# Attention with 32 narrow heads: the joined row maxima transposed one pair of units later, and the last units played four at a time

## Chip, cores and metric

The kernel runs on one core of one Trainium2 chip. The metric is device time of one execution in microseconds (us); smaller is better. Each time named "median" is over three executions of the same program.

## What is computed

A transformer block on one sequence of S = 2048 rows and D = 512 columns, all in float32: attention with 32 heads of width 16, then a gated MLP with a 2048 x 2048 mixing matrix. Only the first part bears on the change:

```python
h = x + A(layernorm(x))            # attention with a full softmax
h2 = h + B(layernorm(h))           # gelu, layernorm, w_sp @ z2, gate, w_out
# A: q, k, v = split(x @ wqkv) into 32 heads of 16 columns
scores = einsum("bhqd,bhkd->bhqk", q, k) * 16 ** -0.5
o = einsum("bhqk,bhkd->bhqd", softmax(scores), v)
return o @ wo
```

## The kernel before, in words

Everything before the line `with ExitStack() as at` (L673) projects x to q, k and v and writes them to scratch memory in DRAM; everything after L872 is the end of the attention's output product for most rows and the MLP. Between them lies the attention proper, on which the change works.

**Units and pairs.** A *unit* is four heads (one `hg` of 8), 512 queries (one `qb` of 4) and 128 keys (one `kb` of 16): 8 x 4 x 16 = 512 units in all. The loop at L826 takes two units at a time, a *pair*. Sixteen units, 8 pairs, share one `hg` and `qb`; I call them a *group* (g = 0 to 31) and number its pairs by their *place*, 0 to 7. A unit needs two score tiles of 128 x 1024, each from two matmuls that sit in the two halves of TensorE's rows (`scores_of`, L688, matmul L700), one exponential per tile on ScalarE (L706), and then `weigh` (L711, matmul L717): the product of the exponentials with v, four heads side by side in the four column strips of TensorE, added into the one PSUM bank `pv`. After the 16th unit `gather` (L721) copies `pv` out and sends it off with eight DMAs.

**Maxima.** The softmax subtracts the row maximum. It is not subtracted on an engine: two extra rows of the queries' tile `qst[g]`, rows 48 and 49 of each half, hold the negated maximum in two parts, two rows of ones stand against them in `kst`, and so the score matmul (50 rows deep) yields scores with the maximum already taken off. So no score matmul of group g can run before these rows are in `qst[g]`. They are made well ahead, by `max_pair` (L215): per step 8 matmuls (L233) into three PSUM banks, six reductions (L238) and one combined reduction (L247) on VectorE, and one absolute value (L243) on ScalarE. Eight such steps make the maxima of one group; one step goes into each pair but for places 0 and 1, of which the first is given two and shares them with the second. LEAD = 11 steps are made before the loop, so the pair at place 4 of group g holds the eighth step of group g+1.

When the eighth step is done, `end` (L249) joins the maxima: one reduction on VectorE (L251), and a split into two parts on GpSimd (L98, L101). Later `max_rows` (L273) transposes the parts on VectorE (L277) and writes them into `qst` with eight small DMAs issued by SyncE (L281).

**The order inside a pair** is written out by hand and carried out by `play` (L740). Its engines take their work strictly in the order in which it is written (manual schedule, L825). In the strings (L41 to L44) two S are one score tile: the first issues the matmul of the first row half, the second that of the other half and the exponential. h is one half (256 queries) of the `weigh` of the unit before, V the `weigh` of the pair's first unit, G the `gather`. M, m, v and u with a bank number are steps of the maxima. N runs `end`, if one has been left over by the pair before (`pending`, `ending`); T runs `max_rows`, if `end` has left something in `turned`. Places 0 and 1 use `FIRST_TWO`, which has no N and no T, the very first pair uses `START`, all others `ORDER`.

**The last units.** From n = 490 on there are no maxima left to make. These 11 pairs (L848 to L860) are not played from a string: two score tiles, `weigh` of the unit before, two score tiles, two or three matmuls of h (L635, `more_h`, with all 128 rows and columns of TensorE), `weigh` of the pair's first unit. The 24 matmuls of h belong to the output product of the first two blocks of 128 rows; `load_o` fetches the attention's output for one such block, `split_o` splits it in two parts. The maxima's three PSUM banks are free by then and serve as a third score tile and the accumulator of h (L842 to L844).

Of the kernel before, what the change touches and what calls it, by code (L numbers as in the profile page):

```python
# [19 lines left out]
S = 2048  # L20
D = 512
H = 32
# [4 lines left out]
NB = S // P  # L27
# [10 lines left out]

ORDER = "v2 S S M1 N S h m0 S m1 M2 S S h S M0 u1 T S V M0".split()  # L41
START = "S S S S M2 m1 h v0 M2 S S M1 S S M0 u2 V m0".split()
FIRST_TWO = ["v2 S S M1 S h S m2 M0 h G M1 S S m2 S m0 S V".split(),
             "u2 S S M1 m0 S S h h v2 M1 S S M0 S S M2 u1 V M0".split()]  # L44
# [12 lines left out]
def block_kernel(ctx: ExitStack, tc: tile.TileContext, x, wqkv, wo, w_in, w_sp4, b_sp, w_out, out):  # L57
# [109 lines left out]
    def head(hg, p, t):  # L167
        return 8 * (hg // 2) + 4 * t + 2 * (hg % 2) + p
# [117 lines left out]
    with ExitStack() as pre:  # L286
# [190 lines left out]
        with tc.manual_schedule(engines={E.PE, E.Activation, E.DVE, E.SP}):  # L477
# [91 lines left out]
            for j in range(24):  # L569
                b, n, i = 1 + j // 8, j // 2 % 4, 1 - j % 2  # L570
# [37 lines left out]
    h_rows = [0, 1, 2, HB, HB + 1, HB + 2] + [sb + HB * i for sb in range(3, HB) for i in range(2)]  # L608
    os_, o2s, xrs, hns, hTs = {}, {}, {}, {}, {}

    def load_o(sb):

        c = slice(sb * P, (sb + 1) * P)
        o = e2.tile([P, DB, P], F32, name="o")
        nc.sync.dma_start(o, o_scr[:, c].rearrange("(d p) s -> p d s", p=P))
        rc = e2.tile([P, DB, P], F32, name="rc")
        for d in range(DB):
            nc.sync.dma_start(rc[:, d, :], r_scr[8 * d:8 * d + 8, c].rearrange(
                "h (o s) -> h o s", o=1).to_broadcast([8, DH, P]))
        xrs[sb] = e2.tile([P, D], F32, name="xr", bufs=3)  # L620
        nc.sync.dma_start(xrs[sb], x[c, :])
        nc.gpsimd.tensor_mul(o, o, rc)
        os_[sb] = o

    def split_o(sb, eh="act", el=None):
        o = os_.pop(sb)
        o2s[sb] = [e2.tile([P, DB, P], F32R, name=f"o2{i}", bufs=1) for i in range(2)]
        split(o2s[sb][0], o2s[sb][1], o, eh, el)
# [44 lines left out]
    with ExitStack() as at:  # L673
# [14 lines left out]
        def scores_of(hg, qb, kb, p):  # L688

            q, k = qst[hg * NQ + qb], kst[hg % 2]
            turn[0] += len(later)
            pool = later[0] if later and turn[0] % 3 == 2 else ps_s
            s = pool.tile([P, 2, 512], F32, name="s")

            def product(t):
                r = slice(RG * t, RG * t + KM)
                nc.tensor.matmul(s[:, t, :], k[r, p, kb * P:(kb + 1) * P], q[r, p, :],  # L700
                                 start=True, stop=True)

            def second():
                product(1)
                t = pp.tile([P, 2, 512], F32, name="pt")
                nc.scalar.activation(t, s, AF.Exp, scale=DH ** -0.5)  # L706
                return t

            return lambda: product(0), second

        def weigh(hg, qb, kb, pts, cols=slice(0, 512)):  # L711

            if kb == 0:
                pv[0] = ps_v.tile([P, 512], F32, name="pv")
            for j in range(4):
                c = (4 * kb + j) * VW
                nc.tensor.matmul(pv[0][32 * j:32 * j + 32, cols], vst[hg % 2][:, c:c + 32],  # L717
                                 pts[j % 2][:, j // 2, cols], start=kb == 0,
                                 stop=kb == NB - 1 and cols.stop == 512)

        def gather(hg, qb, pool=sm):  # L721

            o = pp.tile([P, 512], F32, name="o", bufs=1)
            if pool is sm and not later:
                nc.scalar.activation(o, pv[0], AF.Copy)
            else:
                nc.vector.tensor_copy(o[:, :256], pv[0][:, :256])
                if later and pool is sm:
                    nc.vector.tensor_copy(o[:, 256:], pv[0][:, 256:])
                else:  # L730
                    nc.scalar.activation(o[:, 256:], pv[0][:, 256:], AF.Copy)
            cols = slice(qb * 512, (qb + 1) * 512)
            sums = pool.tile([P, 16], F32, name="sums")
            for j in range(4):
                h = head(hg, j % 2, j // 2)
                nc.sync.dma_start(o_scr[h * DH:(h + 1) * DH, cols], o[32 * j:32 * j + DH, :])
                nc.sync.dma_start(sums[32 * j:32 * j + 32, :], o[32 * j + DH:32 * j + VW, :])
            sums_[0] = (hg, cols, sums, pool)

        def play(order, prev, unit):  # L740
# [38 lines left out]
            assert not ending and len(pts) == 4  # L779
            played.append(pts[2:])  # L780

        played, pending = [], []
        steps_of = {kind: [] for kind in "Mmvu"}

# [17 lines left out]
        def more_h(k):  # L802

            for _ in range(k):
                if not pieces:
                    sb = h_rows[len(hns)]
                    acc = later[0].tile([P, 512], F32, name="h")
                    pieces.extend([sb, acc, h_products(sb, acc)])
                sb, acc, products = pieces
                next(products)  # L810
                made[0] += 1
                if made[0] % (3 * DB):
                    continue
                pieces.clear()
                add_h(sb, acc)
                split_o(h_rows[len(hns) + 1], *("pool", "pool") if hns else [None])
                mv, rs = scale_h(sb)
                hns[sb] = e2.tile([P, D], F32, name="hn", bufs=3)
                nc.vector.tensor_scalar(hns[sb], xrs.pop(sb), mv[:, 0:1], rs,
                                        op0=ALU.subtract, op1=ALU.mult)  # L820

        made = [0]
        units = [(hg, qb, kb) for hg in range(HG) for qb in range(NQ) for kb in range(NB)]
        prev, turn, later = None, [2], []
        with tc.manual_schedule(engines={E.PE, E.Activation, E.DVE, E.SP}):  # L825
            for n in range(0, len(units), 2):  # L826
                (hg, qb, kb), (_, _, kb1) = units[n:n + 2]
                if hg + 1 < HG and n % 64 < 24 and n % 4 == 0:
                    load_k(hg + 1, [n % 64 // 4])
                if hg + 1 < HG and n % 64 < 12 and n % 4 == 2:  # L830
                    load_uv(hg + 1, [n % 64 // 4])
                if hg + 1 < HG and n % 64 == 30:
                    load_v(hg + 1)
                if kb == 2 and n // NB + 3 < HG * NQ:
                    load_q(n // NB + 3)
                steps, place = n // 2 + LEAD < 8 * HG * NQ, n % NB // 2
                while m < min(8 * HG * NQ, n // 2 + LEAD + 1 + (not place and n > 0)):
                    for kind, some in max_pair(m, True).items():
                        steps_of[kind].extend(some)
                    m += 1  # L840
                if not steps and not later:
                    maxima.close()  # L842
                    later.append(attn.enter_context(
                        tc.tile_pool(name="ps_l", bufs=1, space=PSUM, side="right")))  # L844
                if steps:
                    play(START if not n else FIRST_TWO[place] if place < 2 < n else ORDER, prev, (hg, qb, kb, kb1))
                    pts1 = played.pop()
                else:  # L848
                    if pending:
                        pending.pop()()  # L850
                    pts = [score(hg, qb, kb, 0), score(hg, qb, kb, 1)]
                    weigh(*prev)
                    if kb == 0:
                        gather(*units[n - 1][:2])
                    pts1 = [score(hg, qb, kb1, 0), score(hg, qb, kb1, 1)]
                    if n >= 490:
                        more_h(2 + (n < 494))
                    weigh(hg, qb, kb, pts)
                    if turned:
                        max_rows()  # L860
                prev = (hg, qb, kb1, pts1)
                if kb == 6 and n > NB:
                    invert()
                if n % 32 == 16 and n < 6 * 32:
                    load_weights(n // 32)
                if n in (476, 482, 492, 504):
                    load_o(h_rows[(476, 482, 492, 504).index(n)])
                if n == 482:
                    split_o(h_rows[0], "pool", "pool")
            weigh(*prev)  # L870
            gather(*prev[:2], e2)
# [6 lines left out]
    def quarter(pool, name, tag):  # L878
        return pool.tile([P, HB, PITCH], F32R, name=name, tag=tag)[:, :, :FC]

    T = {n: [quarter(zc, n, f"{n}_{i}") for i in range(2)]
         for n in ("t3", "t2", "n4", "t1")}
# [175 lines left out]
    with ExitStack() as fin:  # L1058
# [41 lines left out]
        for p in range(HB):  # L1100
# [98 lines left out]
            if last:  # L1199
                t = zc.tile([P, HB * PITCH], F32, name="qz", tag="n4_1")  # L1200
                first = (t[:, :3 * FC].rearrange("p (i c) -> p i c", c=FC),
                         [t[:, (3 + 2 * i) * FC:(5 + 2 * i) * FC] for i in range(2)])
# [91 lines left out]
        prev, nxt = None, (first[0], None, first[1])  # L1294
        for p in range(HB):
            (q, _, z1), last = nxt, p + 1 == HB
            nxt = None if last else fetch(p + 1)
            h = fetch_h(p)
# [55 lines left out]
            prev = top  # L1354
# [36 lines left out]
```

## Time and profile before

| | |
|---|---|
| median of 3 executions | 1857.24 us (1857.11 to 1857.51) |
| the profiled execution | 1857.51 us |
| its span, first to last instruction | 1855.7 us |
| TensorE (PE) busy | 1846.0 us, 99% of the span |
| VectorE (DVE) busy | 1517.2 us, 82% |
| ScalarE (ACT) busy | 1363.0 us, 73% |
| GpSimd (POOL) busy | 226.4 us, 12% |
| granted TensorE clock | 1.000 of full speed |

Times in the views are microseconds from the span's start. PE is TensorE's matmuls, PEld its weight loads, SPq the queue of SyncE, which issues nearly all DMAs; a DMA row on SPq shows the time in which SyncE issues it, not its transfer. "out<-in" names the tile written and those read; "x8" says that eight instructions are merged in the row, and the second number is then the time from the first one's start to the last one's end. A bracket at the end of a row is idle time of that engine just before, and what ended it. Matmuls overlap: the time from one start to the next is what a matmul costs, not its duration. The chain of work is a list of pieces with start and length that follow on each other without a gap, back from the last instruction; a piece is what the end was waiting for at that time.

### The profile page before, as it was taken

Reading aid. Unit: us, or ns where it says so; the run is one execution under the profiler, and the core shown is the slowest. Engines: PE = TensorE matmul, PEld = TensorE weight load, DVE = VectorE, ACT = ScalarE, POOL = GpSimd, SP = SyncE. Lnnn points to the kernel's source line nnn. Section 1 sums busy time; section 2 is a strip of 40 time slices with the busy share of each in tenths; the row PEclk is TensorE's granted clock in tenths of the full one; section 3 lists DMA queues with packets and bytes.
Section 4 is the critical chain, followed back from the end, with each engine's and each line's share of the span. In section 5 each row is a group of like instructions: output and inputs, shape, how many; then the busy total and the mean of one; then the engine's idle time right before and its main releaser. Section 6 shows DMA issues by size and latency. Waiting matters only on the chain.

```text
span 1855.7 us, 35988 instructions
## 1 busy us (share of the span) xinstructions
PE 1846.0 (99%) x13362; PEld 1024.9 (55%) x13362; DVE 1517.2 (82%) x3030; ACT 1363.0 (73%) x1696; POOL 226.4 (12%) x305
## 2 busy tenths in 40 slices
PE   9999999999999999999999999999999999999999
PEld 6776333433334333334333333333437889999998
DVE  6487999999999999999999999999935777877664
ACT  3224999999999999999999999999995444434221
POOL 2241000011010100000000000000000756001111
PEclk9999999999999999999999999999999999999999
DMA  6688111221120121022011112100124554768662
GB/s 190 181 204 200 42 25 28 50 54 29 39 56 17 48 46 25 14 52 40 14 39 36 21 31 49 25 14 14 32 54 116 172 161 167 226 187 263 210 195 90
DMA packets 148759, 160.15 MB, mean 86 GB/s; under 512 B 63096, under 2 KB 93320, under 8 KB 147240
## 3 DMA queue, kind: packets, MB, share of 16 engines
q1 hardware_dynamic: 143800, 146.44, 29.6%
q10 hardware_dynamic: 4752, 11.41, 1.6%
q8 instruction: 105, 1.72, 0.4%
q14 instruction: 70, 0.57, 0.1%
q0 software_dynamic: 32, 0.01, 0.0%
HBM read 101.26 MB, written 55.61 MB: 85 GB/s over the span
## 4 chain that ended last, share of the span: by engine, by line
PE 97%; DVE 1%; ACT 1%; issue 1%; POOL 0%; POOLq 0%; DVEq 0%; ACTq 0%
PE pv L717 29%; PE m L233 22%; PE s L700 15%; PE acc L104 5%; PE acc L106 5%; PE acc L105 5%; PE g L106 4%; PE g L105 4%; PE g L104 4%; PE acc L635 2%; PE tp L1263 1%; PE h L635 0%; PE tp L959 0%; PE acc L1284 0%; PE acc L463 0%
## 5 line engine op out<-in xcount | busy, mean ns | idle before, releaser
L238 DVE TENSOR_REDUCE mx<-m 128x1 f32<-128x512 f32 x1508 | 949.4, 682 | 97.7 <-PE m L233 74.1
L706 ACT ACTIVATE pt<-s 128x1024 f32<-128x1024 f32 x1024 | 1012.8, 1022 | 15.2 <-PE m L233 6.0
L717 PE MATMUL pv<-pt,vst 128*32 128x256 f32 (+1 forms) x6048 | 591.6, 466 | 0.0
L233 PE MATMUL m<-kst,qst 48*128 48x512 f32 x1508 | 580.7, 468 | 0.5
L700 PE MATMUL s<-qst,kst 50*128 50x512 f32 x2048 | 567.8, 426 | 0.4 <-ACT pt L706 0.4
L233 PEld LDWEIGHTS m<-kst,qst 48*128 48x128 f32 x1508 | 236.6, 184 | 344.9 <-DVE mx L238 292.6
L700 PEld LDWEIGHTS s<-qst,kst 50*128 50x128 f32 x2048 | 271.8, 184 | 135.5 <-ACT pt L706 87.1
L717 PEld LDWEIGHTS pv<-pt,vst 128*32 128x32 f32 x6048 | 122.3, 108 | 230.6 <-issue 218.3
L233 PE MATMUL m<-uvs,qst 48*128 48x512 f32 x497 | 227.8, 458 | 0.0
L243 ACT ACTIVATE ab<-m 128x512 f32<-128x512 f32 x248 | 148.2, 598 | 77.3 <-PE m L233 76.5
L247 DVE CUSTOM_DVE_ANT_0 ab<-m,ab 128x512 f32<-128x512 f32 x249 | 169.4, 680 | 10.6 <-ACT pt L706 10.2
L98 POOL CAST mparts<-nm 128x16 fp32r<-128x16 f32 x32 | 6.3, 196 | 885.1 <-DVE nm L251 885.1
L233 PEld LDWEIGHTS m<-uvs,qst 48*128 48x128 f32 x497 | 90.9, 183 | 38.6 <-DVE mx L238 37.5
L899 ACT ACTIVATE ws<-a 128x512 fp32r<-128x512 f32 x80 | 45.8, 621 | 49.3 <-PE g L106 23.8
L978 ACT ACTIVATE z<-acc 128x464 f32<-128x464 f32 (+2 forms) x64 | 27.5, 456 | 62.5 <-PE acc L106 62.5
L104 PE MATMUL acc<-wi,hT 128*128 128x464 f32 (+2 forms) x196 | 72.8, 371 | 0.0
L106 PE MATMUL acc<-wi,hT 128*128 128x464 f32 (+2 forms) x196 | 71.8, 366 | 0.0
L105 PE MATMUL acc<-wi,hT 128*128 128x464 f32 (+2 forms) x196 | 71.6, 365 | 0.0
L900 DVE TENSOR_TENSOR ws<-a,ws 128x512 fp32r<-128x512 f32 x80 | 56.6, 749 | 12.2 <-ACT ws L899 11.9
L96 ACT ACTIVATE part<-acc 128x512 fp32r<-128x512 f32 x32 | 19.1, 596 | 60.9 <-PE acc L106 56.3
L104 PE MATMUL g<-b,ws 128*128 128x344 f32 x192 | 62.6, 326 | 0.0
L899 ACT ACTIVATE ws<-s 128x512 fp32r<-128x512 f32 x32 | 19.4, 631 | 57.7 <-DVE s L919 57.7
(201 smaller groups left out, 2157.2 us busy)
## 6 DMA issues: line engine op xcount, KB each, us to landing
a<-in_w_sp SPq DMA_DIRECT2D x80, 256.0 KB
qst<-q_scr SPq DMA_DIRECT2D x192, 64.0 KB
z_scr<-z ACTq DMA_DIRECT2D x32, 344.0 KB
kst<-k_scr SPq DMA_DIRECT2D x42, 256.0 KB
k_scr<-part SPq DMA_DIRECT2D x16, 512.0 KB
q_scr<-part SPq DMA_DIRECT2D x16, 512.0 KB
z<-z_scr SPq DMA_DIRECT2D x14, 344.0 KB
b<-z_scr SPq DMA_DIRECT2D x24, 172.0 KB
```

The costliest lines, as they stand in the source:

```text
L104: nc.tensor.matmul(ps, lh, rh, start=first, stop=False)
L105: nc.tensor.matmul(ps, lh, rl, start=False, stop=False)
L106: nc.tensor.matmul(ps, ll, rh, start=False, stop=last)
L233: nc.tensor.matmul(acc, q[r, p, c], keys[r, p], start=True, stop=True)
L238: nc.vector.reduce_max(at(t, e if t else e - 1), acc, axis=AX.X)
L243: nc.scalar.activation(ab[0], acc, AF.Abs)
L247: nc.vector.tensor_tensor_reduce(ab[0], acc, ab[0], 0.5, LOW, ALU.add, ALU.max, at(0, 0))
L700: nc.tensor.matmul(s[:, t, :], k[r, p, kb * P:(kb + 1) * P], q[r, p, :], start=True, stop=True)
L706: nc.scalar.activation(t, s, AF.Exp, scale=DH ** -0.5)
L717: nc.tensor.matmul(pv[0][32 * j:32 * j + 32, cols], vst[hg % 2][:, c:c + 32], pts[j % 2][:, j // 2, cols], start=kb == 0, stop=kb == NB - ...
L899: nc.scalar.activation(hi, src, AF.Copy)
L900: (nc.gpsimd if el == "pool" else nc.vector).tensor_sub(lo, src, hi.bitcast(F32))
```

## The change

It has two parts. In `ORDER` the N moves from behind the first M to behind the T. A T comes before the N of the same pair, so the maxima that N joins in one pair are transposed by the T of the next pair. `START` and `FIRST_TWO` stay as they were.

The other part is the last 11 pairs. The first of them, n = 490, keeps its order and takes four matmuls of h (before: three). The 20 units from 492 on are played four at a time by a new function from a string of its own: two score tiles (a unit), `weigh` of the unit before, two score tiles, four matmuls of h in a row, two score tiles, `weigh`, two score tiles, `weigh`, `weigh`. The matmuls of h are 24 in all as before. The loads of the third and fourth block of the attention's output are written after n = 490 and ahead of n = 504 (before: after n = 492 and after n = 504).

```diff
-ORDER = "v2 S S M1 N S h m0 S m1 M2 S S h S M0 u1 T S V M0".split()
+ORDER = "v2 S S M1 S h m0 S m1 M2 S S h S M0 u1 T N S V M0".split()
+
+FOUR = "S S S S V S S S S H H H H S S S S V S S S S V V".split()
...
+        def play_four(at, prev):
+
+            waiting, opened = [prev], []
+            for x in FOUR:
+                if x == "S":
+                    if opened:
+                        pts = waiting[-1][-1]
+                        pts.append(opened.pop()())
+                    else:
+                        if waiting[-1] is prev or len(waiting[-1][-1]) == 2:
+                            waiting.append((*at.pop(0), []))
+                        unit = waiting[-1]
+                        first, second = scores_of(*unit[:3], len(unit[-1]))
+                        first()
+                        opened.append(second)
+                elif x == "V":
+                    unit = waiting.pop(0)
+                    weigh(*unit)
+                    if unit[2] == NB - 1:
+                        gather(*unit[:2])
+                else:
+                    more_h(1)
+            return waiting.pop()
...
-                else:
+                elif n % 4 == 0:
+                    if n == 504:
+                        load_o(h_rows[3])
+                    prev = play_four(units[n:n + 4], prev)
+                elif n < 492:
                     if pending:
                         pending.pop()()
                     pts = [score(hg, qb, kb, 0), score(hg, qb, kb, 1)]
                     weigh(*prev)
-                    if kb == 0:
-                        gather(*units[n - 1][:2])
                     pts1 = [score(hg, qb, kb1, 0), score(hg, qb, kb1, 1)]
-                    if n >= 490:
-                        more_h(2 + (n < 494))
+                    more_h(4)
                     weigh(hg, qb, kb, pts)
                     if turned:
                         max_rows()
-                prev = (hg, qb, kb1, pts1)
+                if steps or n == 490:
+                    prev = (hg, qb, kb1, pts1)
...
-                if n in (476, 482, 492, 504):
-                    load_o(h_rows[(476, 482, 492, 504).index(n)])
+                if n in (476, 482, 490):
+                    load_o(h_rows[(476, 482, 490).index(n)])
```

## The prediction

> **What bounds the kernel now.** I read the page first: which chain of work ended last.
>
> ```profile
> span 1855.7 us, 35988 instructions
> ...
> L706 ACT ACTIVATE pt<-s 128x1024 f32<-128x1024 f32 x1024 | 1012.8, 1022 | 15.2 <-PE m L233 6.0
> ...
> PE 97%; DVE 1%; ACT 1%; issue 1%; POOL 0%; POOLq 0%; DVEq 0%; ACTq 0%
> ```
>
> The chain is TensorE (PE) for 97% of the span. But VectorE and ScalarE are far from idle in the attention, so the next view is the busy time in stretches: one group of eight pairs, and the last units with their first pair.
>
> ```profile
> 1254.66:1293.40 38.74, 38.71 (x326) 15.32 (x322) 35.41 (x68) 35.99 (x42) 0.46 (x3) 1.00 0.07 16
> 1357.00:1402.40 45.40, 45.40 (x296) 13.82 (x294) 8.72 (x26) 41.50 (x44) 4.87 (x6) 1.00 0.18 51
> ```
>
> The columns are the stretch, its length, then the busy time of PE, PEld, DVE, ACT and POOL, the granted clock (1.00), the DMA share and GB/s. A group takes 38.74 us, 4.84 us a pair, and PE has work in 38.71 of them. DVE would be free for 38.74 - 35.41 = 3.33 us, ACT for 2.75 us. So PE in its written order is the bound, and the other two follow within 10%: whatever stops PE here costs time almost in full. In the last units PE again has no gap, ACT has 3.9 us.
>
> **The change, part one: N behind T.** Next I followed one maximum, in the timeline of VectorE:
>
> ```profile
> 1280.63 0.21 DVE L251 TENSOR_REDUCE nm<-mx 128x16 f32<-128x64 f32 x1
> ...
> 1283.29 0.68 DVE L247 CUSTOM_DVE_ANT_0 ab<-m,ab 128x512 f32<-128x512 f32 x1
> 1283.89 0.08 DVE L247 DVE_READ_ACCUMULATOR2_ANT mx<- 128x1 f32 x1
> 1283.89 0.20 DVE L277 STREAM_TRANSPOSE mturned<-mparts 128x32 f32<-128x32 f32 x1
> ...
> 1288.73 0.08 DVE L247 DVE_READ_ACCUMULATOR2_ANT mx<- 128x1 f32 x1
> ```
>
> N's reduction (L251) and T's transposition (L277) stand in one pair, place 5: N early, T directly behind that pair's u1 (L247). Both are cheap and neither waits: there is no bracket behind them. The u1 of place 6 ends at 1288.73, so with T one pair later the transposition starts 1288.73 - 1283.89 = 4.84 us later. What does it hand on?
>
> ```profile
> 1284.13 5.32 SPq L281 DMA_DIRECT2D qst<-mturned  x8
> 1296.99 0.31 SPq L736 DMA_DIRECT2D o_scr<-o  x1
> ```
>
> ```profile
> L281 SPq DMA_DIRECT2D qst<-mturned x256: 610/610/1226, 147.0 to 1363.5; - x128
> ```
>
> Eight DMAs, issued one behind the other in 5.32 us; the last issue (0.61 us by the median of its line) starts 5.32 - 0.61 = 4.71 us after the first. They fill the two rows of `qst` without which no score matmul of the next group may start. SyncE then has nothing to do until the next group's gather at 1296.99 (L736). The first scores of that next group are at place 0, here in TensorE's weight loads:
>
> ```profile
> 1293.38 0.18 PEld L233 LDWEIGHTS m<-kst,qst 48*128 48x128 f32 x1 [0.84 <-DVE mx L238]
> 1293.38 0.18 PEld L233 LDWEIGHTS m<-uvs,qst 48*128 48x128 f32 x1
> 1293.49 0.28 PEld L700 LDWEIGHTS s<-qst,kst 50*128 50x128 f32 x2
> ```
>
> ```profile
> PEld s L700 <- ACT pt L706: 87.1, 210, 0.7
> ```
>
> M0 (L233, from `kst`) ends place 7, v2 (from `uvs`) and the first two S (L700) open place 0. The second view says that a score matmul's waits (there for a free score tile) are met at its weight load, so the rows must have landed by 1293.49: 1293.49 - 1284.13 = 9.36 us after the first issue. With T a pair later 9.36 - 4.84 = 4.52 us are left, less than the 4.71 us to the last issue alone. So the scores become late, and PE, which takes its work in order, stands with M1, m2, M0, both h and everything else of the pair behind them. DVE has then only the last M0 to reduce and ACT one absolute value; both run dry.
>
> How late depends on one price that the trace does not show: the time from the start of such an issue to its landing. The nearest rows are the first load of x, whose reader waits for it, the last store, whose landing ends the span, and the one DMA for which the page gives the time itself:
>
> ```profile
> 0.75 1.33 SPq L309 DMA_DIRECT2D xg<-in_x  x3
> ...
> 2.93 0.43 DVE L344 BATCH_NORM_STATS2 st<-xg 128x6 f32<-128x256 f32 x1 [1.79 <-DMA xg<-in_x]
> ```
>
> ```profile
> 1852.77 0.37 ACTq L1292 DMA_DIRECT2D out_y<-y  x1
> ```
>
> ```profile
> bias<-in_b_sp POOLq DMA_DIRECT2D x1, 8.0 KB, 2.9
> ```
>
> 2.93 - 0.75 = 2.18 us for a load into on-chip memory from the same queue; 1855.7 - 1852.77 = 2.93 us for the store, with the program's end in it; 2.9 us for bias. Below all of them lies the issue itself, 0.61 us, since nothing lands before it is issued. I take 2.18: same queue, same kind of target, and a reader that was waiting. Landing is then 4.71 + 2.18 = 6.89 us after the first issue, 6.89 - 4.52 = 2.37 us too late; by the ends it is 0.80 and 3.12 us. [...]
>
> Can the pairs behind make it up? They would have to be shorter, and PE idles 0.03 us in a group. What a drained DVE and ACT save is a few waits at weight loads, most of which lie under a V as the 0.84 us above does. I give back 0.1 us: 2.27 us a group. Ends: nothing, and all of it (a rival below).
>
> How often? The eighth step of a group is made at place 4 of the group before, N and T follow at 5 and 6, always in `ORDER`. The maxima of group 0 are transposed before the loop, those of group 31 at n = 490 outside `ORDER`; 32 x 8 = 256 DMAs fit the count above. So 30 groups: 30 x 2.27 = **68.1 us**. Other groups look the same; two more, far from this one:
>
> ```profile
> 237.09 5.31 SPq L281 DMA_DIRECT2D qst<-mturned  x8
> 242.45 2.20 SPq L191 DMA_DIRECT2D raw<-v_scr  x2
> 249.95 0.32 SPq L736 DMA_DIRECT2D o_scr<-o  x1
> ...
> 275.86 5.32 SPq L281 DMA_DIRECT2D qst<-mturned  x8
> 288.72 0.31 SPq L736 DMA_DIRECT2D o_scr<-o  x1
> ```
>
> From the first issue to the gather it is 12.86 us in all three. The queue holds two neighbours: k's loads, written before place 6 in some groups, are then issued ahead of the eight, in SyncE's idle time; v's (L191) now come behind them, and are wanted only a head group later. N itself costs 0.21 us of DVE in either position, behind u1 as well as behind M1, and POOL has all of the next pair for the split; I cost it at nothing, with 0.06 us a group (4.85 against 4.81 and 4.82 for the pairs behind it would be the whole effect) as the end on the good side:
>
> ```profile
> 1278.90:1283.75 4.85, 4.85 (x46) 1.89 (x42) 4.46 (x10) 4.47 (x6) 0.46 (x3) 1.00 0.01 2
> 1283.75:1288.56 4.81, 4.81 (x46) 1.85 (x42) 4.47 (x10) 4.46 (x6) 0.00 (x0) 1.00 0.01 2
> 1288.56:1293.38 4.82, 4.82 (x44) 1.87 (x40) 4.37 (x9) 4.46 (x6) 0.00 (x0) 1.00 0.02 5
> ```
>
> **Part two: four units at a time.** Here the chain in order of time is the bill, PE alone:
>
> ```profile
> 1356.92 0.47 PE s L700 x4
> ...
> 1359.05 0.89 PE h L635 x3
> ...
> 1366.80 0.66 PE s L700 x4
> 1367.46 0.66 PE h L635 x2
> 1368.12 1.00 PE pv L717 x8
> ...
> 1399.97 2.43 PE pv L717 x16
> 1402.40 0.59 PE tp L959 x4
> ```
>
> A unit's scores cost 0.66 us, a V 1.00, two products of h 0.66, three 0.89. So one more costs 0.23, and 0.66 - 0.46 = 0.20 us goes with opening the stretch. A pair with two is 4 pieces beside h: 2 x 0.66 + 2 x 1.00 + 0.66 = 3.98 us, four units 7.96. New: four times 0.66, three V at 1.00, four h in one stretch at 0.66 + 2 x 0.23 = 1.12, and a V right behind a V, which saves its own opening:
>
> ```profile
> 1295.51 0.64 PE L717 MATMUL pv<-pt,vst 128*32 128x256 f32 x8
> ...
> 1299.35 1.07 PE L717 MATMUL pv<-pt,vst 128*32 128x256 f32 x16
> ```
>
> Two h alone are 2 x (0.64 - 0.07 of overlap) = 1.14, two together 1.07 - 0.07 = 1.00: 0.14 saved, so the fourth V costs 0.86. Sum 2.64 + 3.00 + 1.12 + 0.86 = 7.62 us, 0.34 less. ACT must keep up: four exponentials in a row take 3.77 us,
>
> ```profile
> 1381.60 3.77 ACT L706 ACTIVATE pt<-s 128x1024 f32<-128x1024 f32 x4 [0.22 <-PE s L700]
> ```
>
> so with 1.02 us each they start (3.77 - 1.02) / 3 = 0.92 us apart, eight need 7.36 us: under 7.62, PE stays the bound with 0.26 us to spare. Inside a four the exponentials of a unit are through before its V: the nearest is the last unit, whose second one ends some 0.2 us after the two V. Whole stretch before: 1402.40 - 1356.92 = 45.48 us. After: first pair 4.02 + 0.23 = 4.25, five fours 38.10, last V 1.0 + 0.2: 43.55. **About 1.9 us less**; 0 if ACT's last quarter of a microsecond is used up by waits, and no more than 45.48 - 4.25 - 5 x 7.36 - 1.2 = 3.2 if PE's stretches shrank to ACT's rate. The loads that moved keep their neighbours on SyncE's queue (the third block stays behind the last eight L281, the fourth behind the sums of n = 502), and the second block's products now end some five microseconds before the stretch does, which covers the additions and the split behind them.
>
> **Sum**, on the profiled execution's 1857.51 us: 1857.5 + 68.1 - 1.9 = 1923.7, say **1924 us**, 3.6% slower. The median of the runs shown is 1857.24; I keep the profiled one.
>
> **Rivals.**
> *The delay is made up, or never arises* (not slower). The place is the eight pairs of a group; the price is 2.27 us in each, so it is undone where a pair runs in 4.84 - 2.27 / 8 = 4.56 us. DVE with 35.41 / 8 = 4.43 and ACT with 4.50 us would allow that; PE, at 38.71 of 38.74 us busy, speaks against it, unless its busy time hides waits (ends of matmuls are modelled). Then only part two is left: 1857.5 - 1.9 = 1855.6, within 0.2%, which is about what a measurement of this kernel can tell from no change. The same time comes out if T still fell into N's pair, the change not doing what it says; the strings say otherwise. Together 4%.
> *The clock falls as well.* If PE's clock dropped to half after each standstill and stayed so for the pair at place 0, that pair would cost up to 4.82 us more per group; for half of it, 2.4 x 30 = 72 us, the time is 1996. The clock column says 1.00 in every stretch, but no stretch of the attention has such a standstill, so the trace cannot exclude it: 5%. [...]
> *The DMAs land early*: near the low end, under 1 us late, leaves 1857.5 + 30 x 0.8 - 1.9 = 1880: 6%.
> The forecast with its own bounds has the other 85%.
>
> **How the numbers follow.** Delays from 1.3 us (between the low end and the row I take) to 3.12 us give 1857.5 + 39 - 1.9 = 1895 to 1857.5 + 94 - 1.9 = 1949; range 1895 to 1950. Slower by over 0.2% are the forecast, the clock and the early landing, 85 + 5 + 6 = 96%. The undoing's 4% is within 0.2% for 3 and faster by more for 1, where N's 0.06 us a group comes on top of part two.
>
> **What would show it.** After: weight loads of L700 wait for a DMA into `qst` some 30 times, about 70 us in all; a group takes 41.0 instead of 38.74 us with PE at 38.7 busy; from the first L281 to the gather's first L736 it is 10.3 instead of 12.86 us; the last stretch takes 43.6 us. If the groups still take 38.7 us, or PE waits there for something else, part one is wrong; a clock under 1.00 at place 0 is the second rival.

## The result, and the profile after

The changed kernel takes 1970.65 us (median of 6 executions, 1961.87 to 1981.05) against 1857.49 us: a ratio of 1.0613, 95% interval 1.0575 to 1.065, so 6.1% slower. Forecast were 1924 us and a range of 1895 to 1950. The profiled execution took 1965.98 us, its span is 1964.2 us. The page first (lines of the source have moved by 2 in the attention, so L283 is the old L281, L702 the old L700):

```profile
span 1964.2 us, 35987 instructions
...
DVE  6588877887888788877887888888773666867664
...
PEclk9999989998999899989998989999899999999999
...
PE 84%; SPq 6%; DVE 5%; DMA 2%; issue 2%; ACT 1%; POOL 0%; DVEq 0%; POOLq 0%; ACTq 0%
```

The two rows by slices (the span in 40 equal parts, each digit a share in tenths) were before:

```profile
DVE  6487999999999999999999999999935777877664
...
PEclk9999999999999999999999999999999999999999
```

New is this. The chain of work, PE for 97% before, now goes through SyncE's queue, VectorE and a DMA for 13%. VectorE, full in every slice of the attention before, has slices of seven tenths. And the granted clock falls below nine tenths in some slices of the attention, and only there; its mean is 0.967, before 1.000.

The queue of SyncE shows how long the groups take, from the start of one row of eight DMAs to the next:

```profile
242.89 5.32 SPq L283 DMA_DIRECT2D qst<-mturned  x8
...
289.30 5.33 SPq L283 DMA_DIRECT2D qst<-mturned  x8
299.38 0.31 SPq L738 DMA_DIRECT2D o_scr<-o  x1
...
332.83 5.32 SPq L283 DMA_DIRECT2D qst<-mturned  x8
...
373.56 5.29 SPq L283 DMA_DIRECT2D qst<-mturned  x8
```

46.41, 43.53 and 40.73 us, where it was 38.74. Of the 29 such distances in the attention, 17 lie between 40.49 and 40.87 us (median 40.60), the others between 43.53 and 46.44; before, the median of the 29 is 38.77 us. From the first L283 to the gather it is 10.08 us (12.86 before). TensorE's weight loads and matmuls at place 0 of the group that begins behind the DMAs of 289.30:

```profile
293.71 0.18 PEld L235 LDWEIGHTS m<-uvs,qst 48*128 48x128 f32 x1
295.11 0.18 PEld L702 LDWEIGHTS s<-qst,kst 50*128 50x128 f32 x1 [1.21 <-ACT ab L245]
295.74 0.19 PEld L702 LDWEIGHTS s<-qst,kst 50*128 50x128 f32 x2 [0.45 <-DMA qst<-mturned]
```

```profile
293.71 0.50 PE L235 MATMUL m<-kst,qst 48*128 48x512 f32 x1
293.72 0.50 PE L235 MATMUL m<-uvs,qst 48*128 48x512 f32 x1
295.14 1.11 PE L702 MATMUL s<-qst,kst 50*128 50x512 f32 x3 [0.92 <-DMA qst<-mturned]
296.08 0.39 PE L235 MATMUL m<-kst,qst 48*128 48x512 f32 x1
```

Before, the same scores and the M1 behind them were:

```profile
1293.72 0.41 PE L700 MATMUL s<-qst,kst 50*128 50x512 f32 x2
1293.96 0.40 PE L233 MATMUL m<-kst,qst 48*128 48x512 f32 x1
```

The standstill is the one forecast, with its releaser by name. (The first weight load's wait is put down to ACT, which was done at the time; its matmul beside it names the DMA.) The two scores, side by side before, now come one behind the other, 0.63 us apart by their weight loads (the seventh and the eighth DMA are issued 0.65 us apart), and M1 starts at 296.08, 6.78 us after the first issue. Before it was 9.83 us after it, with the transposition 4.84 us earlier: 6.78 - 9.83 + 4.84 = 1.79 us late.

The clock is the other half. Busy times by stretches of the same place, and by whole groups (columns as in the prediction; the clock is the third number from the end):

```profile
294.00:295.00 1.00, 0.22 (x2) 0.00 (x0) 0.69 (x1) 0.60 (x1) 0.00 (x0) 1.00 0.02 3
295.00:296.00 1.00, 0.72 (x3) 0.44 (x4) 0.00 (x0) 0.00 (x0) 0.00 (x0) 1.00 0.01 2
296.00:297.00 1.00, 1.00 (x13) 0.23 (x11) 0.50 (x1) 0.67 (x1) 0.00 (x0) 1.00 0.00 0
297.00:298.00 1.00, 1.00 (x11) 0.45 (x11) 0.67 (x2) 0.80 (x2) 0.00 (x0) 0.79 0.00 0
298.00:299.00 1.00, 1.00 (x10) 0.38 (x4) 0.81 (x2) 0.82 (x2) 0.00 (x0) 0.50 0.00 0
...
304.00:305.00 1.00, 1.00 (x15) 0.35 (x16) 1.00 (x4) 1.00 (x2) 0.00 (x0) 0.80 0.09 16
305.00:306.00 1.00, 1.00 (x16) 0.54 (x10) 0.33 (x1) 0.75 (x1) 0.00 (x0) 1.00 0.14 29
```

```profile
242.89:289.30 46.41, 45.16 (x324) 17.61 (x322) 35.87 (x67) 36.42 (x41) 1.51 (x4) 0.85 0.15 25
289.30:332.83 43.53, 42.45 (x324) 16.56 (x322) 35.68 (x67) 36.41 (x41) 3.89 (x5) 0.92 0.09 26
332.83:373.56 40.73, 39.48 (x324) 15.50 (x322) 35.50 (x67) 36.15 (x41) 0.47 (x3) 1.00 0.23 51
```

PE idles 1.06 us between 294 and 296. When it has work again, its clock falls to one half, from within the slice at 297 to within that at 304. The group with the full clock takes 40.73 us, with PE idle for 1.25; the two others have PE idle for 1.25 and 1.08 us and a clock of 0.85 and 0.92 in the mean.

The last units, in the chain in order of time:

```profile
1466.73 0.47 PE s L702 x4
...
1473.29 1.12 PE h L637 x4
...
1476.74 1.85 PE pv L719 x16
...
1507.31 3.31 PE pv L719 x24
1510.62 0.59 PE tp L987 x4
```

Four products of h cost 1.12 us and two V in a row 1.85, as forecast; the whole stretch takes 1510.62 - 1466.73 = 43.89 us instead of 45.48.

So the sum for the profiled executions is: up to the last units 1466.73 - 1356.92 = 109.8 us more, in them 1.6 less, behind them 0.3 more (453.6 against 453.3), together 108.5 = 1965.98 - 1857.51. The 30 groups at 1.83 us (40.60 - 38.77, the medians) make 54.9 of the 109.8. The other 54.9 are left for the clock. Counted directly, the 12 long distances exceed 40.60 us by 52.6 us together; a 13th group with half clock begins behind the last of them. (The expectations below take 1.85 us a group.)

### The profile page after: what moved, and what is told of

Read it like the earlier page. It is cut to its first block, busy times and chain, and to the rows that moved or that the text cites. A ratio compares the mean times of both kernels' runs of the same rounds, so it can differ in the third digit from the quotient of the medians.

```text
span 1964.2 us, 35987 instructions
## 1 busy us (share of the span) xinstructions
PE 1919.4 (98%) x13362; PEld 1051.1 (54%) x13362; DVE 1522.3 (78%) x3030; ACT 1370.9 (70%) x1696; POOL 225.8 (11%) x305
## 4 chain that ended last, share of the span: by engine, by line
PE 84%; SPq 6%; DVE 5%; DMA 2%; issue 2%; ACT 1%; POOL 0%; DVEq 0%; POOLq 0%; ACTq 0%
PE pv L719 24%; PE m L235 18%; PE s L702 13%; SPq L283 6%; PE acc L106 5%; PE acc L108 5%; PE acc L107 5%; PE g L108 3%; PE g L107 3%; PE g L106 3%; DVE mx L240 3%; DMA qst<-mturned 2%; PE acc L637 2%; DVE ab L249 1%; PE tp L1291 0%
## 5 line engine op out<-in xcount | busy, mean ns | idle before, releaser
L702 PE MATMUL s<-qst,kst 50*128 50x512 f32 x2048 | 601.5, 445 | 34.7 <-DMA qst<-mturned 22.0
L719 PE MATMUL pv<-pt,vst 128*32 128x256 f32 (+1 forms) x6048 | 615.1, 484 | 0.0
L235 PE MATMUL m<-kst,qst 48*128 48x512 f32 x1508 | 602.8, 484 | 0.5
L235 PEld LDWEIGHTS m<-kst,qst 48*128 48x128 f32 x1508 | 248.7, 192 | 348.5 <-DVE mx L240 300.8
L702 PEld LDWEIGHTS s<-qst,kst 50*128 50x128 f32 x2048 | 288.9, 193 | 186.4 <-ACT pt L708 89.1
L235 PE MATMUL m<-uvs,qst 48*128 48x512 f32 x497 | 234.1, 471 | 0.0
L928 DVE TENSOR_TENSOR ws<-a,ws 128x512 fp32r<-128x512 f32 x80 | 56.4, 748 | 13.3 <-ACT ws L927 13.2
L108 PE MATMUL g<-t,ws 128*128 128x344 f32 x192 | 61.3, 319 | 0.0
```

The lines of the kernel that those rows point to most:

```text
L108: nc.tensor.matmul(ps, ll, rh, start=False, stop=last)
L235: nc.tensor.matmul(acc, q[r, p, c], keys[r, p], start=True, stop=True)
L928: (nc.gpsimd if el == "pool" else nc.vector).tensor_sub(lo, src, hi.bitcast(F32))
```

## The experiments

Theory A: the whole loss is the late maxima. TensorE stands at place 0 of 30 groups, and after some of these standstills its clock is halved. Rival B: N at the pair's end disturbs VectorE and the clock. Rival C: the units played four at a time cost the time. All eight kernels were run in two sets, with medians of 3 to 11 executions, each beside the kernel before, at 1857.19 and 1856.95 us. The ratios take in all these executions and so differ a little from those of the medians.

**N alone.** The string of the changed kernel in the kernel before.

```diff
-ORDER = "v2 S S M1 N S h m0 S m1 M2 S S h S M0 u1 T S V M0".split()
+ORDER = "v2 S S M1 S h m0 S m1 M2 S S h S M0 u1 T N S V M0".split()
```

> Only N moved behind T; the last units as before. Theory A (the whole loss is the late maxima: TensorE stands at place 0 of 30 groups and its clock is halved after some of these): 1857.5 + 110 us of the stretch of the groups, 1967 us, clock about 0.967, the stretch of the last units back at 45.5 us. Rival C (the units played four at a time cost the time): below 1900 us.

Measured 1967.65 us (median of three, 1966.86 to 1981.17; a fourth execution took 1997.1 us at a clock of 0.950), ratio 1.0617 (1.0586 to 1.0648), clock 0.959 in the profiled execution, one of 1981.17 us; a pair of the last units takes 3.98 us as before. The loss is in this string; C falls.

**The fours alone.** The changed kernel with the old string.

```diff
-ORDER = "v2 S S M1 S h m0 S m1 M2 S S h S M0 u1 T N S V M0".split()
+ORDER = "v2 S S M1 N S h m0 S m1 M2 S S h S M0 u1 T S V M0".split()
```

> N at its old place, the last units four at a time. Theory A: 1857.5 - 1.6 = 1856 us, clock 1.000, last stretch 43.9 us instead of 45.5 us. Rival C: over 1900 us.

Measured 1855.52 us, ratio 0.9992 (0.9983 to 1.0001), clock 1.000, last stretch 43.88 us. The stretch is shorter as forecast; by the times alone the gain can't be told from no change. Its median is the lowest of this study.

**T early.** N stays at the pair's end, T goes to the front of the next pair.

```diff
-ORDER = "v2 S S M1 S h m0 S m1 M2 S S h S M0 u1 T N S V M0".split()
+ORDER = "v2 S S M1 T S h m0 S m1 M2 S S h S M0 u1 N S V M0".split()
```

> As the changed kernel, but T stands behind the first M of the pair after N, some 3.2 us earlier. Theory A: the eight DMAs land before the scores need them (their margin was -1.8 us), no standstill, no halved clock: 1855 to 1856 us, a group 38.7 us, clock 1.000. Rival B (it is N at the pair's end, ahead of the last M0 on VectorE, that costs time and clock): as the changed kernel, 1960 us or more.

Measured 1856.2 us, ratio 0.9994 (0.9985 to 1.0002), clock 1.000. N at the pair's end and T in the next pair are both still there, and nothing is lost: B falls. It is the 3.2 us by which T comes sooner that decide. (N's new place brings nothing either: the fours alone are as fast.)

**The standstill filled.** Ahead of the first score of a group at place 0, 14 matmuls that need no maxima are put into the score tile that the scores then overwrite. They add work and leave the output as it is.

```diff
+FILL = 14
...
-        def scores_of(hg, qb, kb, p):
+        def scores_of(hg, qb, kb, p, fill=0):
...
+            for i in range(fill):
+                r = slice(RG * (i % 2), RG * (i % 2) + KS)
+                nc.tensor.matmul(s[:, i % 2, :], k[r, p, kb * P:(kb + 1) * P], k[r, p, :512],
+                                 start=True, stop=True)
...
-                        first, second = scores_of(hg, qb, kbs[k], p)
+                        first, second = scores_of(hg, qb, kbs[k], p, FILL if kbs[0] == 0 and not pts and hg + qb else 0)
```

> As the changed kernel, with 14 matmuls of 512 columns put ahead of the first score of each group at place 0, on keys against keys and into the score tile that the scores then overwrite: they need no maxima, so TensorE works (some 1.6 us) where it stood. Theory A with the standstill as the cause of the clock: the wait stays, the clock stays at 1.000: 1857.5 + 30 x 1.85 - 1.6 = 1911 us, up to 1918 if the fillers end late. If the clock falls for another reason than the standstill: 1965 us and a clock of 0.967.

Measured 1910.64 us (1910.44 to 1912.32), ratio 1.0289 (1.0275 to 1.0303), clock 1.000. The matmuls of one group's end and start, and a whole group in the view by stretches:

```profile
247.44 0.50 PE L236 MATMUL m<-kst,qst 48*128 48x512 f32 x1
247.44 0.49 PE L236 MATMUL m<-uvs,qst 48*128 48x512 f32 x1
247.77 1.78 PE L703 MATMUL s<-kst 48*128 48x512 f32 x14
249.38 0.76 PE L708 MATMUL s<-qst,kst 50*128 50x512 f32 x3
```

```profile
283.69:324.21 40.52, 40.50 (x338) 16.79 (x336) 35.49 (x67) 36.12 (x41) 3.88 (x5) 1.00 0.10 28
```

The scores are as late as in the changed kernel and a group still takes 40.6 us (median of 29; 40.52 the one shown), but PE is busy in all of it and the clock never falls. With 14 x 30 = 420 more matmuls the kernel is 60 us faster than the changed one. This separates the two costs: 1910.64 - 1857.19 + 1.6 = 55 us are the delay, the other 60 us the clock, and the clock's cause is the standstill.

**T ahead of u1, T ahead of M0, T at the end.** Three more places of T, to vary the delay.

```diff
-ORDER = "v2 S S M1 S h m0 S m1 M2 S S h S M0 u1 T N S V M0".split()
+ORDER = "v2 S S M1 S h m0 S m1 M2 S S h S M0 T u1 N S V M0".split()   # ahead of u1
+ORDER = "v2 S S M1 S h m0 S m1 M2 S S h S T M0 u1 N S V M0".split()   # ahead of M0
+ORDER = "v2 S S M1 S h m0 S m1 M2 S S h S M0 u1 S V M0 T N".split()   # at the end
```

> As the changed kernel, T one token earlier, ahead of u1: the transposition and its DMAs start 0.69 us sooner, so a group loses 1.85 - 0.69 = 1.16 us and TensorE idles about 0.5 us instead of 1.2. Theory A with the clock halved by any standstill: 1857.5 - 1.6 + 35 us and the clock still about 0.97, 1945 us. Theory A with a standstill that must be long enough for the clock: 1891 us, clock 1.000.

> As the changed kernel, T two tokens earlier, ahead of M0 and u1: the DMAs start about 1.3 us sooner. Theory A: a group loses 0.5 to 0.6 us, 1857.5 - 1.6 + 16 = 1872 us, clock 1.000.

> As the changed kernel, T and N at the very end of the pair, behind M0: the DMAs start about 0.65 us later. Theory A: a group loses 2.5 us (75 us in all), TensorE idles 1.8 us instead of 1.2, and the clock is halved after more of the standstills than in the changed kernel: above 1985 us, about 2010, clock below 0.96. If the clock's fall does not depend on the standstill's length: 1857.5 - 1.6 + 75 + 54 = 1985 us, clock 0.967.

| T | us (lowest to highest) | ratio (interval) | clock | group at full clock | groups with half clock | us at half clock |
|---|---|---|---|---|---|---|
| ahead of M0 | 1876.8 (1875.31 to 1877.93) | 1.0105 (1.009 to 1.012) | 0.998 | 39.38 us | 1 | 7 |
| ahead of u1 | 1910.0 (1899.57 to 1925.51) | 1.0291 (1.0228 to 1.0354) | 0.984 | 39.96 us | 6 | 61 |
| behind u1 (the change) | 1970.65 (1961.87 to 1981.05) | 1.0613 (1.0575 to 1.065) | 0.967 | 40.60 us | 13 | 130 |
| at the end | 2069.16 (2067.91 to 2070.61) | 1.1142 (1.1125 to 1.1158) | 0.929 | none | all | 294 |

The clock and the last three columns are of each profiled execution; the group at full clock is the median. The waits of the score matmuls for their maxima, ahead of u1 and at the end (total, times, longest):

```profile
PE s L702 <- DMA qst<-mturned: 8.6, 30, 0.5
```

```profile
PE s L702 <- DMA qst<-mturned: 49.1, 41, 2.3
```

The delays came out as expected: 39.38 - 38.77 = 0.61 us (0.5 to 0.6) and 1.19 us (1.16). For the clock neither expectation for u1 was right: standstills of 0.5 to 1.0 us still halve it, but in 6 groups only. In five of the six PE idles in two pieces, each under 0.5 us as in the view and together 0.50 to 0.64 us; in the sixth it is 0.97 us in one piece, which the profile puts down to ACT. At the end the clock is halved in every group, and the time is 59 us above what I had guessed; the delay is 2.9 us there, not 2.5 (the shortest groups, 44.6 us, hold one stretch of 6.8 us at half clock, which costs 43.57 - 40.60 = 2.97 us by the medians of the changed kernel: 44.6 - 2.97 - 38.77 = 2.9).

**Two queues.** T as in the change, but four of the eight DMAs issued by GpSimd.

```diff
-                nc.sync.dma_start(
+                (nc.gpsimd if j else nc.sync).dma_start(
```

> As the changed kernel, T where the change has it, but four of the eight DMAs are issued by GpSimd, four by SyncE. Theory A with the issues one behind the other as the larger part of the delay: SyncE's four land 2.0 + 1.9 = 3.9 us after the transposition, GpSimd's four about 5 us after, against 4.8 us that are there: 1856 to 1865 us, clock 1.000. Rival (the delay is mostly one landing, whatever stands before it): 1900 us or more.

Measured 1863.05 us (1859.01 to 1867.42), ratio 1.0032 (1.0021 to 1.0043), clock 0.997. The usual group takes 38.77 us: with half the issues on another queue the maxima are in time, although T is where the change put it. The row of eight issues is what makes a pair's delay too much. Of what is left above the kernel before, the larger part in the profiled execution (1864.44 us) is one group in which GpSimd issued late, 3.20 us after SyncE where it is 0.27 or 0.62 us in the other groups of the attention:

```profile
1251.86 2.70 SPq L283 DMA_DIRECT2D qst<-mturned  x4
1255.06 2.25 POOL L283 DMA_DIRECT2D qst<-mturned  x4 [7.50 <-DVE mx L240]
```

```profile
1258.57 0.50 PE L702 MATMUL s<-qst,kst 50*128 50x512 f32 x2 [1.55 <-DMA qst<-mturned]
```

The wait was 1.55 us, the clock stayed halved for 10 us, and the group took 45.35 us. Why GpSimd was late there I did not try.

## Why the prediction was wrong, point by point

**The bound** held: nothing behind a standstill made it up. A group at full clock is 40.6 us long, and DVE and ACT are busy for as long as before (35.50 and 36.15 against 35.41 and 35.99 us).

**The mechanism of part one** was right: place, cause, releaser and the number of groups. T at an earlier place or with its DMAs on two queues takes the delay away. One sign was misjudged: some 70 us of waits for these DMAs were named, and the profile after puts 22.0 us down to them at the matmuls:

```profile
PE s L702 <- DMA qst<-mturned: 22.0, 34, 1.4
```

PE stands only 1.0 to 1.4 us in a group. Most of the rest of the delay goes by with the scores running one behind the other: in the group shown M1 starts 0.94 us after the first score (296.08 - 295.14), before 0.24 us (1293.96 - 1293.72).

**The size of the delay** was a little off: 2.27 us forecast, 1.83 measured. The term is the landing. I took 2.18 us from the load of x. The eighth issue of the group shown starts 4.71 us after 289.30, at 294.01, and its score's weights load at 295.74: at most 1.73 us. In the whole sum this is 30 x 0.44 = 13.2 us too much.

**The clock** is the step that failed: the sum of the forecast had it at nothing. "The clock falls as well" stood among the rivals at 5%, at 2.4 us a group and 1996 us; it happens, in 13 of 30 groups, for 54.9 us in all or 1.8 us a group. With the measured sizes the sum is 1857.5 + 54.9 + 54.9 - 1.6 = 1966 us, the profiled execution's time. I had let the trace's silence (1.00 in every stretch, and no standstill in any) carry the chance; that a standstill leaves the clock alone was shown by no run. What the runs showed: the filled kernel, with PE busy in the same place, keeps a clock of 1.000 where the changed kernel has 0.967, so the standstill is the cause, and with T ahead of u1 0.50 to 0.64 us were enough in five groups. A sum that makes an engine stand 30 times should have had the clock, which its own trace could not exclude, among its likely cases, and the range up to 1996.

**Part two** was right to 0.3 us: 1.6 us less instead of 1.9; a four takes 7.63 us (7.62 forecast), from 1486.28 to 1493.91 in the chain for instance. The first pair takes 4.25 us as forecast; most of the difference is the last V, 3.31 - 1.85 = 1.46 us instead of 1.2. It is too small for the times to show.

**The range** (1895 to 1950) missed because it left the clock out; its rival's 1996 and the 1924 without it enclose the result.

## What to carry to other kernels

Where one engine works without a gap, count the margin of each small DMA behind it in time, not in steps: the last of eight issues starts 4.71 us after the first, before any landing, and a step later by one pair (4.84 us) turned 3.0 us of margin into 1.83 us of delay in every group. Here TensorE's standstills of 1.0 to 1.4 us a group cost as much again through the clock (delay and clock 54.9 us each), so price a wait twice. And where a wait can't be avoided, try issuing work in it that needs no new data: here 14 useless matmuls a group made the late kernel 60 us faster (1910.64 against 1970.65 us).

## What the runs showed of the hardware

**When the clock is halved.** In the changed kernel's profiled execution the falls of the granted clock lie at 249.80, 297.58, 461.42, 509.21, 673.05, 840.30 us and seven more; any two of the 13 differ by a multiple of 3.4133 us to within 0.02 (first and last by 1191.25 us, 349 times 3.4133), and the clock stays at half for 6.83, 10.24 or 13.65 us, two, three or four times 3.4133 (17.07, five times, at 421.2, 469.0 and 1237.0 us of the run of N alone and at 1444.3 us of the one with T at the end). So in this trace all changes of the clock in the attention lie on one grid of 3.413 us. One such stretch:

```profile
297.58:304.41 6.83, 6.83 (x31) 2.72 (x30) 4.19 (x8) 4.13 (x5) 0.00 (x0) 0.50 0.09 17
```

Which standstills were followed by half clock went by their place in this grid: the 11 that began 0.05 to 1.71 us after an edge all were, from the next edge on; of the 19 that began 1.85 us or later two were, the longest of all (1.39 us) and one that reached 0.6 us into the next interval. The standstills are 0.9 to 1.4 us long, and in the group shown M1 runs again 1.86 us after the stop (294.22 to 296.08). Why the place counts was not shown. The trace with T ahead of u1 agrees: of its 15 standstills of 0.5 us or more in all, five of the six that began 0.19 to 0.42 us after an edge were followed by half clock, and none of the nine that began 1.81 us or later; of the 15 shorter ones one was, the longest of them (0.499 us). So in these two traces both length and place went with it. This was read from traces, not varied by itself. The place in the grid may also be why the times of the changed kernel scatter by 1%: its six executions go from 1961.87 us at a clock of 0.969 to 1981.05 us at 0.959, so the scatter comes with the clock, while the filled kernel and the one with T at the end, where none or all of the standstills halve the clock, scatter by 0.1% like the kernel before. That the groups meet the grid otherwise each time was not shown. What sets two, three, four or five intervals stays open.

**What a microsecond at half clock costs.** The 12 long distances of the changed kernel hold 122.9 us at half clock and exceed 40.60 us by 52.6 us together: 0.43 us each, not 0.5. Why it is less than half was not measured.

**Landing of a small DMA.** Of 2 KB from on-chip to on-chip memory, at most 1.73 us from the start of its issue in the group shown, less than the 2.18 us of the 128 KB load that I had taken.
